# A three-part kernel on one core: the compare of a float64 cast moved to its first steps, and steps among the expert units laid out anew

## The chip, the cores and the metric

The kernel runs on one core of a Trainium2 chip. The core has a matrix engine (PE, whose weight loads are listed as PEld), a vector engine (DVE), an activation engine (ACT) and a general engine (POOL), which run side by side, each through its own list of instructions in order, and wait for each other by semaphores. A fifth one (SP) issues nearly all DMA transfers, also in order. The metric is the device time of one execution in microseconds (us), lower is better.

## The reference

The computation has three parts, one behind the other:

```python
# 1: attention in chunks of 32 queries over 56 keys near them and 8 memory keys (4 batches, 8 heads, 768 positions, 64 wide)
a = np.exp(scores - np.max(scores, axis=-1, keepdims=True)); a = a / (np.sum(a, axis=-1, keepdims=True) + 1e-09)
out[:, :, c_start:c_end] = np.matmul(a, v_full)
# 2: soft mixture of 8 experts with 4 slots each, x is 3072 x 512
logits = x @ phi
d = softmax(logits, axis=0);  slot_input = d.T @ x
h = np.maximum(slot_input[e] @ w1[e], 0.0);  slot_out[e] = h @ w2[e]       # for each expert e, 512 -> 1024 -> 512
c = softmax(logits, axis=1);  x = c @ slot_out
# 3: a layer with a soft gate and a normalisation
h = x @ w_in                                  # w_in is drawn in float64, 512 x 1024
solu = h * softmax(h);  ln = (solu - mean) / np.sqrt(var + 1e-06) * g_ln
return (ln @ w_out).astype(np.float32)        # w_out is drawn in float64, 1024 x 512
```

`softmax` is written out in the reference as in the first part. `w_in` and `w_out` come to the chip as float64, in 16 chunks of 512 KB, and are made into float32 there.

## The kernel before, in words

**Stages.** The first loop goes over 32 groups `g` of attention (two heads, half a batch). In each, PE multiplies queries and keys (L237), DVE takes maxima and differences (L255, L260), ACT the exponential (L269), PE turns the result (L274), ACT copies it (L277), PE multiplies with the values (L297), DVE divides (L263). POOL, ACT and DVE spread keys and values into padded buffers (`move`, L281 to L285). Every four groups one block of tokens is complete, and its logits, the running column maximum and the slot inputs follow (`emit_lg` to `emit_dacc`, L316 to L369). The second loop goes over 32 *units* `n`: one unit is half of an expert's first product (`emit_w1`, L447, eight matmuls) or of its second (`emit_w2`, L465, eight matmuls). The third stage turns the slots into the layer's 24 blocks of tokens and ends in long rows of products (L680, L690).

**A unit.** ACT copies a first product out (L448), PE turns it (L454), DVE adds up parts (L457), POOL applies the relu (L458); this is `emit_ht`, and it stands behind the first product of the next expert half, two units later. The second product of that half comes three units after its turn. Each unit uses two weight chunks of 512 KB. Weights flow into some 27 slots; `load_e` issues what fits, and `release` returns a slot when its last reader has been issued.

**A cast.** One float64 chunk is 128 x 512 pairs of words. From the high word, DVE shifts the exponent and mantissa bits into float32 form (`bits`, L523), puts in sign and top exponent bit (`more`, L529) and keeps the power of two alone (`power`, L534); ACT turns the low word into a number (L526) and squares the high word read as float32 (L535); POOL multiplies low word and power (L538 or L542) and adds (L539 or L545); DVE sets the result to zero where the square is under a threshold (`flush`, L552). For `w_out` ACT then scales by `g_ln` and rounds to the high part (L569), and DVE takes the rest as a low part (L573). Six of the eight `w_in` chunks are cast in the attention loop, one step a group (`casts`), a seventh around its end (`tail`), the eighth and all of `w_out` in the second loop: a new cast starts every three units (`LANE`), and each unit does the next step of every cast begun (`lane`).

**The combine weights.** The row softmax of the logits is done in four batches `b` of six blocks (`combine`). Its steps are: maximum and difference (DVE L405, POOL L406), exponential (ACT L409), sum, inverse and product (DVE L412 to L414, POOL L415), a rounded high part (ACT L418; for the first batch with a turn of its own, DVE L388, PE L392, ACT L393), the low part (POOL L422), and turns on PE with ACT's copies (`emit_c4t`, L438, L439). The list `cb` holds them, one step a unit from unit `SIDE`; each batch's turn is put `CLATE` places further down.

**Order.** Every engine does its instructions in the order in which the program emits them; a step that waits holds all that stand behind it on its engine. Within a unit that is: the unit's product, the turn of an earlier one, the cast steps, SP's loads, a combine step.

Of the kernel before, what the change touches and what calls it, by code (L numbers as in the profile page):

```python
# [12 lines left out]
ACTF = mybir.ActivationFunctionType  # L13
ALU = mybir.AluOpType
# [27 lines left out]
CAST0, CASTN, NEARLY = 3, 4.5, 6  # L42
VLEAD = 3
LOADS = [0] + [1, 1, 1, 0] * 8
LANE, SIDE = 3, 2
C_ID, C_I4, C_REP, C_NM, C_PHI, C_G = 0, 128, 160, 288, 289, 417
NCONST = 425
NPE, NZ = 4, 4
# [11 lines left out]
SPL = 3  # L60
LAG = 2

CLATE = 2
TORD = [1, 0]
TKEEP = [2, 1]
KEEP = (4, 2, 0, 10)
# [5 lines left out]
TINY = (2.0 ** -15 * 1.125) ** 2  # L72
# [3 lines left out]
def tile_kernel(ctx: ExitStack, tc: tile.TileContext, kr, vr, w1, w2, w_in, w_out, cst, out):  # L76
    nc = tc.nc
    pe, dve, act, pool, sp = nc.tensor, nc.vector, nc.scalar, nc.gpsimd, nc.sync
# [9 lines left out]
    def area(tag, regions):  # L88

        total = 0  # L90
        for name, n in regions:
            total = (total + 31) // 32 * 32
            arenas[name] = [total, n, None]
            total += n
        tl = sb.tile([P, total], FP32, name=regions[0][0] + "_area", tag=tag)
        for name, _ in regions:
            arenas[name][2] = tl
# [16 lines left out]
    def at(name, off, n, dt=FP32):  # L114
        o, size, tl = arenas[name]
        assert off + n <= size, (name, off, n, size)
        v = tl[:, o + off:o + off + n]
        return v if dt == FP32 else v.bitcast(dt)
# [3 lines left out]
    def bank(i):  # L122
        return banks[i]
# [32 lines left out]
    w_in_f = at("win", 0, KC * FF)  # L156
# [41 lines left out]
    slot_of = {}  # L198
# [6 lines left out]
    def load_e(n=99):  # L205
        while n and nxt[0] < len(chunks):
            key = chunks[nxt[0]]
            if key[0] == "wout":
                slot = wslot[key[1]]
            elif free:  # L210
                slot = free.pop(0)
            else:
                break
            slot_of[key] = slot
            if key[0] in ("w1", "w2"):
                src = (w1 if key[0] == "w1" else w2)[key[1], key[2]]
                sp.dma_start(out=slot.rearrange("p (k f) -> p k f", k=2), in_=src)
            else:
                src = (w_in if key[0] == "win" else w_out)[key[1]]
                sp.dma_start(out=slot.bitcast(I64), in_=src)  # L220
            nxt[0] += 1
            n -= 1

    def release(key):
        free.append(slot_of[key])
# [169 lines left out]
    def combine(b):  # L395

        l = L[:, TB * b:TB * b + TB, :]
        m, z = cm[:, TB * (b % 2):TB * (b % 2) + TB], cs[:, TB * (b % 2):TB * (b % 2) + TB]
        l2 = l.rearrange("p t (o s) -> p t o s", o=1).to_broadcast([P, TB, 2, NSLOT])

        def wide(x):
            return x.rearrange("p (t o) -> p t o", o=1).to_broadcast([P, TB, NSLOT])

        def top():
            dve.tensor_reduce(out=m, in_=l, axis=AX.X, op=ALU.max)  # L405
            pool.tensor_tensor(out=l, in0=l, in1=wide(m), op=ALU.subtract)  # L406

        def ex():
            act.activation(out=l, in_=l, func=ACTF.Exp)  # L409

        def norm():
            dve.tensor_reduce(out=z, in_=l, axis=AX.X, op=ALU.add)  # L412
            dve.tensor_scalar(out=z, in0=z, scalar1=1e-9, scalar2=None, op0=ALU.add)
            dve.reciprocal(out=z, in_=z)  # L414
            pool.tensor_tensor(out=l, in0=l, in1=wide(z), op=ALU.mult)  # L415

        def hi():
            act.copy(out=c4_of(b)[:, :, 0:2, :], in_=l2)  # L418

        def lo():  # L420
            c4 = c4_of(b)
            pool.tensor_tensor(out=c4[:, :, 2:4, :], in0=l2, in1=c4[:, :, 0:2, :].bitcast(FP32), op=ALU.subtract)  # L422

        return [top, ex, norm, hi if b else lambda: (emit_c0(), hi()), lo, lambda: emit_c4t(b)]
# [25 lines left out]
    def emit_ht(e, half):  # L450
        n = 2 * e + half
        tp = bank(2 + n % 2)
        for j in range(4):
            pe.transpose(out=tp[:, j * P:j * P + P], in_=hr[n % 2][:, j * P:j * P + P], identity=ident)  # L454
        h = ht[e][:, 4 * half:4 * half + 4, SE * e:SE * e + SE]
        parts = tp.rearrange("p (j k s) -> p j s k", j=4, k=KC)[:, :, SE * e:SE * e + SE, :]
        dve.tensor_reduce(out=h, in_=parts, axis=AX.X, op=ALU.add)  # L457
        pool.tensor_scalar(out=h, in0=h, scalar1=0.0, scalar2=None, op0=ALU.max)  # L458
# [11 lines left out]
    def keep_clock(o, n):  # L470

        for _ in range(n):
            pe.matmul(out=o, lhsT=c4t(0), rhs=whi[0], start=True, stop=True)
# [38 lines left out]
            out=m4[:, sl], in0=mhi[:, sl].bitcast(FP32), scalar=nmask, in1=m_of(half), op0=ALU.mult, op1=ALU.add  # L512
        )

    def cast_ops(raw, t2, dst, apart=False):
        w32 = raw.bitcast(I32).rearrange("p (n w) -> p n w", w=2)
        lo = raw.bitcast(U32).rearrange("p (n w) -> p n w", w=2)[:, :, 0]
        lf, hf = (raw.rearrange("p (n w) -> p n w", w=2)[:, :, i] for i in range(2))
        hi = w32[:, :, 1]
        di, t2i = dst.bitcast(I32), t2.bitcast(I32)  # L520

        def bits():
            dve.tensor_scalar(  # L523
                out=di, in0=hi, scalar1=3, scalar2=0x3FFFFFFF, op0=ALU.logical_shift_left, op1=ALU.bitwise_and
            )
            act.activation(out=lf, in_=lo, func=ACTF.Copy, scale=2.0 ** -52)  # L526

        def more():
            dve.scalar_tensor_tensor(  # L529
                out=di, in0=hi, scalar=-0x40000000, in1=di, op0=ALU.bitwise_and, op1=ALU.bitwise_or  # L530
            )

        def power():
            dve.tensor_scalar(out=t2i, in0=di, scalar1=-0x800000, scalar2=None, op0=ALU.bitwise_and)  # L534
            act.activation(out=hf, in_=hf, func=ACTF.Square)  # L535

        def low(eng=pool):
            eng.tensor_tensor(out=t2, in0=lf, in1=t2, op=ALU.mult)  # L538
            eng.tensor_tensor(out=dst, in0=dst, in1=t2, op=ALU.add)  # L539

        def low_a():
            pool.tensor_tensor(out=t2, in0=lf, in1=t2, op=ALU.mult)  # L542

        def low_b():
            pool.tensor_tensor(out=dst, in0=dst, in1=t2, op=ALU.add)  # L545

        def flush(eng=dve):
            if eng is pool:
                pool.tensor_scalar(out=hf, in0=hf, scalar1=TINY, scalar2=None, op0=ALU.is_ge)
                pool.tensor_tensor(out=dst, in0=hf, in1=dst, op=ALU.mult)  # L550
                return
            dve.scalar_tensor_tensor(out=dst, in0=hf, scalar=TINY, in1=dst, op0=ALU.is_ge, op1=ALU.mult)  # L552

        return [bits, more, power] + ([low_a, low_b] if apart else [low]) + [flush]

    def win_ops(j, t):

        sl = slice(512 * j, 512 * j + 512)
        ops = cast_ops(slot_of["win", j], at("tmp", 512 * (t % 2), 512), w_in_f[:, sl], apart=True)
        return ops[:-1] + [lambda: (ops[-1](), release(("win", j)))]  # L560

    def wout_ops(j, t):

# [191 lines left out]
    with tc.manual_schedule():  # L755
# [67 lines left out]
        emit_lcopy(HB - 2)  # L823
        emit_softmax(GROUPS + 2)
        tail = win_ops(NEARLY, NEARLY)
        tail[0]()
        tail[1]()
# [26 lines left out]
            f()  # L854
        load_e()
        cb = [x for b in range(NTILE // TB) for x in combine(b)]
        cb.append(lambda: None)
        for i in range(5, len(cb), 6):
            x = cb.pop(i)
            cb.insert(i + CLATE, x)  # L860
        area("x1", [("wo2", 3 * DM)])
# [8 lines left out]
        after = []  # L870
        lane = []
        waiting = [lambda t, j=j: win_ops(j, t) for j in range(NEARLY + 1, 2 * KC)]
        waiting += [lambda t, j=j: wout_ops(j, t) for j in range(FC)]
        for n, u in enumerate(units):
            if u == units[-1]:
                keep_clock(bank(5), KEEP[0])
            (emit_w1 if u[0] == "w1" else emit_w2)(*u[1:])
            after.append(u[1:] if u[0] == "w1" else None)
            if len(after) > 1 and after[-2] and (LAG == 1 or after[-2][0] == 0):
                emit_ht(*after[-2])  # L880
            if LAG == 2 and len(after) > 2 and after[-3] and after[-3][0]:
                emit_ht(*after[-3])
            for j in range(2):
                release(u[:2] + (2 * u[2] + j,))
            if n % LANE == 0 and waiting:
                lane.append(waiting.pop(0)(n // LANE))
            for q in list(lane):
                q.pop(0)()
                if not q:
                    lane.remove(q)  # L890
            load_e()
            if n >= SIDE and cb:
                cb.pop(0)()
# [108 lines left out]
```

## Time and profile before

| what | value |
|---|---|
| runs | 351.29 us median of 3 (350.53 to 351.62) |
| profiled execution | 351.6 us, its span 349.8 us |
| busy: PE, DVE, ACT, POOL | 308.8, 249.1, 238.9, 221.1 us |
| PE's last block of work (L680) | 130.4 us |
| HBM | 80.11 MB read, 16.78 MB written |

The span runs from the first to the last instruction. Times in the views are from the span's start. A duration holds what an instruction waited for within itself; a time in brackets is idle time of the engine before it, with what ended it. The attention loop and its tail go to 124 us, the 32 units to 189 us, and the third stage to the end.

### The profile page before, as it was taken

How to read it: one execution, taken by the hardware profiler on the slowest of the kernel's cores; microseconds unless marked ns; L12 is line 12 of the kernel's file. 1: busy time of each engine (PE TensorE's matmuls, PEld its weight loads, DVE VectorE, ACT ScalarE, POOL GpSimd, SP SyncE). 2: the span in 40 equal slices, each digit the busy share in tenths (PEclk: the TensorE clock that was granted, in tenths of full speed). 3: DMA queues.
4: the chain of work that ended last, by engine and by line, in shares of the span. 5: the costliest groups of instructions: out<-in, count | busy, mean ns of one | idle time of the engine just before them, and what ended most of it. 6: DMA issues, size and time to landing. Idle time of an engine off the chain costs nothing.

```text
span 349.8 us, 8154 instructions
## 1 busy us (share of the span) xinstructions
PE 308.8 (88%) x2968; PEld 215.8 (62%) x2968; DVE 249.1 (71%) x445; ACT 238.9 (68%) x437; POOL 221.1 (63%) x413
## 2 busy tenths in 40 slices
PE   2988799899988796756769999999999999999996
PEld 1765566666665341221224578888888888888885
DVE  4696988989897754765732598686988698788540
ACT  2678777977875553554642578987998789799631
POOL 5588797886984256587671056787667477567600
PEclk9999999999999999999969999999999999999999
DMA  7999999999999999999910001576665766576621
GB/s 275 414 414 414 413 408 415 407 389 382 334 414 412 418 379 410 415 420 417 410 42 3 0 0 75 197 238 214 207 248 176 258 219 246 195 259 212 240 90 60
DMA packets 38919, 97.41 MB, mean 278 GB/s; under 512 B 4320, under 2 KB 14944, under 8 KB 38880
## 3 DMA queue, kind: packets, MB, share of 16 engines
q1 hardware_dynamic: 38736, 96.68, 72.6%
q8 instruction: 23, 0.38, 0.4%
q10 hardware_dynamic: 144, 0.22, 0.3%
q14 instruction: 16, 0.13, 0.1%
HBM read 80.11 MB, written 16.78 MB: 277 GB/s over the span
## 4 chain that ended last, share of the span: by engine, by line
PE 58%; DVE 14%; POOL 11%; ACT 6%; DMA 6%; issue 3%; SPq 0%; POOLq 0%; ACTq 0%; DVEq 0%
PE bank L680 35%; DMA kq_area<-in_kr_dram 6%; PE h L592 3%; PE bank L297 3%; POOL cst_area L538 2%; POOL hr_area L458 2%; PE bank L447 2%; POOL wo_area L539 2%; POOL v_area L285 2%; PE bank L465 2%; DVE wo_area L552 1%; PE bank L316 1%; PE bank L237 1%; PE bank L358 1%; DVE cst_area L529 1%
## 5 line engine op out<-in xcount | busy, mean ns | idle before, releaser
L680 PE MATMUL bank<-wh_area,yh_area 128*128 128x512 f32 x552 | 130.4, 391 | 0.0
L680 PEld LDWEIGHTS bank<-wh_area,yh_area 128*128 128x128 f32 x552 | 103.4, 188 | 22.4
L285 POOL TENSOR_SCALAR v_area<-v_area 64x780 f32<-64x780 f32 x64 | 57.1, 892 | 17.2 <-issue 5.3
L663 DVE STREAM_TRANSPOSE yq_area<-yq_area 128x1024 f32<-128x1024 f32 x20 | 24.9, 1245 | 23.0 <-DMA yq_area<-z 23.0
L237 PE MATMUL bank<-kq_area 128*32 128x128 f32 x768 | 29.5, 290 | 8.2 <-ACT kq_area L281 6.8
L297 PE MATMUL bank<-v_area,s_area 128*32 128x130 f32 x768 | 28.5, 281 | 8.9 <-ACT s_area L277 3.3
L646 POOL TENSOR_SCALAR cst_area<-cst_area 128x1 f32<-128x1 f32 x72 | 27.9, 388 | 7.1
L607 DVE SCALAR_TENSOR_TENSOR eb_area<-h,eb_area 128x1024 f32<-128x1024 f32 x24 | 28.8, 1203 | 4.5 <-ACT eb_area L601 4.2
L598 DVE TENSOR_REDUCE cst_area<-h 128x1 f32<-128x1024 f32 x24 | 29.0, 1216 | 3.9 <-PE h L592 3.9
L645 POOL TENSOR_SCALAR cst_area<-cst_area 128x1 f32<-128x1 f32 x72 | 25.6, 356 | 7.7
L670 ACT CAST yh_area<-yq_area 128x1024 fp32r<-128x1024 f32 x20 | 21.0, 1050 | 13.3 <-DVE yq_area L663 13.1
L297 PEld LDWEIGHTS bank<-v_area,s_area 128*32 128x32 f32 x768 | 20.3, 110 | 14.4 <-POOL v_area L285 4.7
L237 PEld LDWEIGHTS bank<-kq_area 128*32 128x32 f32 x768 | 20.3, 114 | 14.1 <-ACT kq_area L281 9.1
L601 ACT ACTIVATE eb_area<-h,cst_area 128x1024 f32<-128x1024 f32 x24 | 26.6, 1108 | 1.3 <-DVE cst_area L598 1.3
L630 ACT ACTIVATE eb_area<-eb_area,cst_area 128x1024 f32<-128x1024 f32 x24 | 27.3, 1138 | 0.1
L281 ACT COPY kq_area<-kq_area 64x512 f32<-64x512 f32 x39 | 23.7, 608 | 5.3 <-DMA kq_area<-in_kr_dram 5.0
L674 DVE TENSOR_TENSOR yh_area<-yq_area,yh_area 128x1024 fp32r<-128x1024 f32 x20 | 24.6, 1228 | 2.3 <-ACT yh_area L670 2.3
L627 ACT ACTIVATE eb_area<-eb_area,cst_area 128x1024 f32<-128x1024 f32 x20 | 23.1, 1155 | 2.4 <-DVE eb_area L607 1.3
L255 DVE TENSOR_REDUCE cst_area<-bank 128x6 f32<-128x384 f32 x32 | 17.6, 551 | 8.5 <-PE bank L237 8.4
L636 POOL TENSOR_SCALAR cst_area<-cst_area 128x1 f32<-128x1 f32 x24 | 6.3, 264 | 23.7 <-ACT eb_area L630 23.1
L311 ACT COPY s_area<-bank 128x384 f32<-128x384 f32 x32 | 15.2, 478 | 7.5 <-PE bank L308 7.5
L269 ACT ACTIVATE s_area<-s_area 128x384 f32<-128x384 f32 x32 | 16.9, 527 | 3.9 <-DVE s_area L260 3.7
(151 smaller groups left out, 600.8 us busy)
## 6 DMA issues: line engine op xcount, KB each, us to landing
e_area<-in_w_dram SPq DMA_DIRECT2D x42, 512.0 KB, 9.9
kq_area<-in_kr_dram SPq DMA_DIRECT2D x32, 448.0 KB, 6.8
v_area<-in_vr_dram SPq DMA_DIRECT2D x32, 390.0 KB, 7.2
ex_area<-in_w_dram SPq DMA_DIRECT2D x22, 512.0 KB, 9.9
z<-eb_area SPq DMA_DIRECT2D x20, 512.0 KB, 3.0
yq_area<-z SPq DMA_DIRECT2D x80, 128.0 KB, 2.8
out_dram<-eb_area SPq DMA_DIRECT2D x23, 256.0 KB, 2.1
e_area<-in_w_in_dram SPq DMA_DIRECT2D x8, 512.0 KB, 8.2
```

The source lines that it names most:

```text
L237: pe.matmul(out=bk[32 * j:32 * j + 32, t * 128:(t + 1) * 128], lhsT=kq[i][:, KS + c * CH:KS + (c + 1) * CH], rhs=kwin(g % 2, c), start=Tru ...
L285: pool.tensor_scalar(out=o, in0=i, scalar1=1.0, scalar2=0.0, op0=ALU.mult, op1=ALU.add)
L297: pe.matmul(out=bk[32 * j:32 * j + 32, t * 2 * VW:(t + 1) * 2 * VW], lhsT=atb[g % 2][:, c * CH:(c + 1) * CH], rhs=vz[g % 2][:, :, c * VW:( ...
L598: dve.tensor_reduce(out=sc("nm", i), in_=fin["h"][i % 2], axis=AX.X, op=ALU.max, negate=True)
L601: act.activation(out=eb[i % FIN], in_=fin["h"][i % 2], func=ACTF.Exp, bias=sc("nm", i), accum_out=sc("s", i))
L607: dve.scalar_tensor_tensor(out=ub[i % FIN], in0=fin["h"][i % 2], scalar=-1.0 / FF, in1=eb[i % FIN], op0=ALU.mult, op1=ALU.mult, accum_out= ...
L630: act.activation(out=sq, in_=ub[i % FIN], func=ACTF.Square, scale=-float(FF), bias=sc("nu", i), accum_out=sc("vs", i))
L645: pool.tensor_scalar(out=t, in0=r, scalar1=r, scalar2=xx, op0=ALU.mult, op1=ALU.mult)
L646: pool.tensor_scalar(out=r, in0=t, scalar1=1.5, scalar2=r, op0=ALU.add, op1=ALU.mult)
L663: dve.transpose(out=yv[i % FIN].rearrange("p (f a t) -> p a f t", f=FC, a=4), in_=yq[i % FIN].rearrange("p (a f t) -> p a f t", f=FC, a=4),)
L674: dve.tensor_tensor(out=yl[i % FIN][:, sl], in0=tps(i, sl) if i < NPE else yv[i % FIN], in1=yh[i % FIN][:, sl].bitcast(FP32), op=ALU.subtract,
L680: pe.matmul(out=fin["o"][i % 2], lhsT=a[i % FIN][:, f * 128:(f + 1) * 128], rhs=w[f], start=start, stop=stop)
```

## The change

- In a cast, ACT squares the high word first, into the place of the result, and DVE's compare, now the second step, sets the high word itself to zero or keeps it. The bits are taken from that word after. The power of two is taken in the same step as sign and top bit. The last step is POOL's addition; `w_in`'s slot is returned after POOL's product. The number of instructions is the same.
- In the second loop each cast step has its unit written down: `CASTU` gives the units after the cast's first in which the steps are issued. The two DVE steps and POOL's product share the fourth; the scaling stands two units after POOL's addition.
- The combine steps start in unit 1 instead of 2, and a batch's turn stands three places further down instead of two. With the filler steps the last turn is in unit 26 as before.

```diff
-LANE, SIDE = 3, 2
+LANE, SIDE = 3, 1
+
+CASTU = (0, 1, 2, 3, 3, 4, 6, 7)
-CLATE = 2
+CLATE = 3
...
-    def cast_ops(raw, t2, dst, apart=False):
+    def cast_ops(raw, t2, dst):
...
+        def square():
+            act.activation(out=dst, in_=hf, func=ACTF.Square)
+
+        def flush():
+            dve.scalar_tensor_tensor(out=hf, in0=dst, scalar=TINY, in1=hf, op0=ALU.is_ge, op1=ALU.mult)
+
         def bits():
...
-
-        def power():
             dve.tensor_scalar(out=t2i, in0=di, scalar1=-0x800000, scalar2=None, op0=ALU.bitwise_and)
-            act.activation(out=hf, in_=hf, func=ACTF.Square)
...
-        def flush(eng=dve):
...
-            dve.scalar_tensor_tensor(out=dst, in0=hf, scalar=TINY, in1=dst, op0=ALU.is_ge, op1=ALU.mult)
-
-        return [bits, more, power] + ([low_a, low_b] if apart else [low]) + [flush]
+        return [square, flush, bits, more, low_a, low_b]
...
-        ops = cast_ops(slot_of["win", j], at("tmp", 512 * (t % 2), 512), w_in_f[:, sl], apart=True)
-        return ops[:-1] + [lambda: (ops[-1](), release(("win", j)))]
+        ops = cast_ops(slot_of["win", j], at("tmp", 512 * (t % 2), 512), w_in_f[:, sl])
+        return ops[:4] + [lambda: (ops[4](), release(("win", j)))] + ops[5:]
...
-        cb.append(lambda: None)
-        for i in range(5, len(cb), 6):
+        cb += [lambda: None] * (CLATE - 1)
+        for i in range(5, 24, 6):
             x = cb.pop(i)
             cb.insert(i + CLATE, x)
...
             if n % LANE == 0 and waiting:
-                lane.append(waiting.pop(0)(n // LANE))
-            for q in list(lane):
-                q.pop(0)()
-                if not q:
-                    lane.remove(q)
+                for i, f in enumerate(waiting.pop(0)(n // LANE)):
+                    lane.append((n + CASTU[i], f))
+            for x in [x for x in lane if x[0] == n]:
+                x[1]()
+                lane.remove(x)
```

## Rows read from the trace of the kernel before

**Rows 1.** The page's slices, 40 equal ones: the granted clock, GB/s.

```profile
PEclk9999999999999999999969999999999999999999
GB/s 275 414 414 414 413 408 415 407 389 382 334 414 412 418 379 410 415 420 417 410 42 3 0 0 75 197 238 214 207 248 176 258 219 246 195 259 212 240 90 60
```

**Rows 2.** The chain that ended last: start, length, what.

```profile
22.85 8.58 DMA kq_area<-in_kr_dram
...
149.89 1.11 POOL cst_area L538
...
321.79 18.86 PE bank L680 x83
```

**Rows 3.** PE's waits, 123.9 to 189.6: total us, times, longest.

```profile
PE bank L438 <- POOL hr_area L422: 6.9, 4, 2.6
PE bank L454 <- ACT hr_area L448: 4.8, 3, 1.6
PE bank L392 <- DVE hr_area L388: 2.9, 1, 2.9
PE bank L465 <- POOL hr_area L458: 2.7, 6, 0.7
```

**Rows 4.** Two rounds: busy us (instructions) by engine, granted clock, DMA share, GB/s.

```profile
141.47:154.15 12.68, 8.54 (x67) 3.04 (x66) 7.65 (x18) 6.82 (x14) 9.07 (x10) 1.00 1.03 417
154.15:166.83 12.68, 8.55 (x68) 3.05 (x67) 7.65 (x18) 6.87 (x14) 9.07 (x10) 1.00 1.02 417
```

**Rows 5.** DVE's cast steps in order of time: start, duration, line, what.

```profile
149.42 0.41 DVE L523 TENSOR_SCALAR wo_area<-w_area 128x512 int32<-128x512 int32 x1
...
152.38 1.47 DVE L552 SCALAR_TENSOR_TENSOR cst_area<-w_area,cst_area 128x512 f32<-128x512 f32 x1 [2.54 <-POOL cst_area L539]
153.76 0.68 DVE L529 SCALAR_TENSOR_TENSOR wo_area<-w_area,wo_area 128x512 int32<-128x512 int32 x1
...
154.76 0.41 DVE L534 TENSOR_SCALAR cst_area<-wo_area 128x512 int32<-128x512 int32 x1
...
158.97 0.69 DVE L552 SCALAR_TENSOR_TENSOR wo_area<-w_area,wo_area 128x512 f32<-128x512 f32 x1 [2.42 <-POOL wo_area L539]
...
180.16 0.74 DVE L573 SCALAR_TENSOR_TENSOR wh_area<-cst_area,wh_area 128x512 fp32r<-128x512 f32 x1
```

**Rows 6.** POOL in order of time.

```profile
146.23 0.24 POOL L458 TENSOR_SCALAR hr_area<-hr_area 128x16 f32<-128x16 f32 x1
...
148.92 0.96 POOL L458 TENSOR_SCALAR hr_area<-hr_area 128x16 f32<-128x16 f32 x1
...
151.08 1.27 POOL L539 TENSOR_TENSOR cst_area<-cst_area 128x512 f32<-128x512 f32 x1
152.30 0.99 POOL L422 TENSOR_TENSOR hr_area<-cst_area,hr_area 128x384 fp32r<-128x384 f32 x1
154.78 0.75 POOL L406 TENSOR_TENSOR cst_area<-cst_area 128x192 f32<-128x192 f32 x1 [1.49 <-DVE cst_area L405]
...
161.11 0.52 POOL L415 TENSOR_TENSOR cst_area<-cst_area 128x192 f32<-128x192 f32 x1 [1.96 <-ACT w_area L535]
```

**Rows 7.** PE near the end of the units.

```profile
178.68 1.54 PE L438 MATMUL bank<-cst_area,hr_area 128*128 128x128 f32 x6 [2.65 <-POOL hr_area L422]
...
188.43 1.06 PE L465 MATMUL bank<-e_area,hr_area 128*32 128x512 f32 x8
```

**Rows 8.** Stretches of 4 us, columns as in rows 4.

```profile
60.00:64.00 4.00, 4.00 (x74) 3.02 (x78) 3.92 (x12) 2.87 (x8) 3.71 (x4) 1.00 1.02 401
...
176.00:180.00 4.00, 1.35 (x7) 1.14 (x6) 2.29 (x4) 1.18 (x3) 2.55 (x4) 0.69 0.04 17
180.00:184.00 4.00, 4.00 (x20) 0.88 (x19) 0.90 (x2) 1.32 (x4) 3.28 (x3) 0.50 0.00 0
184.00:188.00 4.00, 3.98 (x28) 1.81 (x27) 1.44 (x4) 1.22 (x2) 0.92 (x2) 0.95 0.02 6
```

**Rows 9.** What SP's queue waited for: total us, times, longest.

```profile
SPq L217 <- DVE cst_area L552: 7.0, 1, 7.0
```

More of the change, by code (lines that the diff above doesn't have):

```diff
@@ L531, in more @@
             )
-        def power():
             dve.tensor_scalar(out=t2i, in0=di, scalar1=-0x800000, scalar2=None, op0=ALU.bitwise_and)
-            act.activation(out=hf, in_=hf, func=ACTF.Square)
-        def low(eng=pool):
-            eng.tensor_tensor(out=t2, in0=lf, in1=t2, op=ALU.mult)
-            eng.tensor_tensor(out=dst, in0=dst, in1=t2, op=ALU.add)
         def low_a():
@@ L545, in low_b @@
             pool.tensor_tensor(out=dst, in0=dst, in1=t2, op=ALU.add)
-        def flush(eng=dve):
[L548 to L551, printed above, removed]
-            dve.scalar_tensor_tensor(out=dst, in0=hf, scalar=TINY, in1=dst, op0=ALU.is_ge, op1=ALU.mult)
-        return [bits, more, power] + ([low_a, low_b] if apart else [low]) + [flush]
+        return [square, flush, bits, more, low_a, low_b]
     def win_ops(j, t):
         sl = slice(512 * j, 512 * j + 512)
-        ops = cast_ops(slot_of["win", j], at("tmp", 512 * (t % 2), 512), w_in_f[:, sl], apart=True)
-        return ops[:-1] + [lambda: (ops[-1](), release(("win", j)))]
+        ops = cast_ops(slot_of["win", j], at("tmp", 512 * (t % 2), 512), w_in_f[:, sl])
+        return ops[:4] + [lambda: (ops[4](), release(("win", j)))] + ops[5:]
     def wout_ops(j, t):
```

## The prediction

> **What bounds the kernel now.** I read the page's slices first, then the chain of waits in order of time, then the stretch in which the chain changes engine most often. Three stages show. In the attention stage, to 124 us, the last load on the chain ends at 31.43 us [rows 2]; from there the chain passes between DVE, ACT, POOL and PE, with DVE busy 3.92 us of 4 [rows 8]. In the last stage PE runs one product behind the other, and its last long piece alone is 18.86 us [rows 2]; the change puts nothing there. Between them lie the 32 expert units, and they end when the last eight matmuls do, at 189.49 us [rows 7].
>
> The expert stage looks like a stage that waits for weights, since loads run at 410 to 420 GB/s through it. But they are over in the slice that begins at 174.9 us with 42 GB/s [rows 1]: 42/415 of 8.745 us is 0.9, so the last lands near 175.8, and PE ends 13.7 us after that. The stage runs on buffered weights, and something else sets its pace.
>
> That is seen in a round of six units (two casts, one batch of combine weights). It takes 12.68 us twice over; PE works 8.54 us of it, DVE 7.65, ACT 6.82, POOL 9.07 [rows 4]. No engine is full, so a loop through several is the bound. PE's waits name it [rows 3]: 6.9 us for POOL's low part of the combine weights (L422), 4.8 for ACT's copy of the first product (L448), 2.9 for the first turn (L388) and 2.7 for POOL's relu (L458), 17.3 together. Behind these is the cast: DVE's compare (L552) waits for POOL's two steps, ACT's scaling for the compare, and the copy that PE needs is behind the scaling in ACT's queue.
>
> A second thing is in the durations. DVE's compare takes 0.69 us at 158.97, but 1.47 at 152.38, where POOL's L422 began 0.08 us before it [rows 5, 6]; it ends 0.56 us after L422's end, so it was held until POOL was nearly done. The other way round POOL's relu takes 0.24 us at 146.23 and 0.96 at 148.92, ending at 149.88, just after DVE's L523, which ended at 149.83. DVE's cast steps and POOL exclude each other. The Trainium skill says the same (SBUF — State Buffer, Who interferes with whom): DVE and GpSimd share a port pair, a DVE instruction with two SBUF inputs or in a two-port mode takes it, and the loser blocks for a whole instruction. The 0.78 us more agree with it.
>
> Last, a clock loss. PE waits 2.65 us until 178.68 [rows 7], and the granted clock is 0.69 in 176 to 180, 0.50 in 180 to 184 and 0.95 in 184 to 188 [rows 8], which is the lower level, 1.2 GHz, until about 184.4. From 178.68 to there PE does 5.7 us at half speed: 2.8 us lost.
>
> **The change part by part.** *The compare first.* A cast has the same eight instructions as before: on DVE 0.41 + 0.68 + 0.41 + 0.69 and, for w_out, 0.74 us [rows 5]; on ACT the square and the low word; on POOL two products. The compare now writes the strided high word, which no row shows. The nearest rows are this kind of instruction with a strided operand on the reading side, 0.68 (L529) and 0.69 (L552); the far ones are 0.41, DVE's shortest cast step, and 1.47, the blocked compare. I take 0.69; at 1.47 four rounds of two casts would cost 6.2 us more, which stays among the two in ten left out. What is gained is order: nothing on DVE waits for POOL's result any more. DVE's wlo waits for ACT's scaling of the unit before. The new wait, compare on square, has a whole unit (2.1 us) or attention group of cover; in the tail, where both are issued together, DVE next has a step that waits for PE anyway. Without cover it is 0.7 us a cast.
>
> *Eight units.* The scaling stands two units after POOL's last step instead of one after a compare that itself waits, so ACT's queue stops there for nothing and the 4.8 us of copy waits should nearly go. What is late next is POOL: the first product is issued in the unit of the two DVE steps that feed it, and the relu of a later unit queues behind it. PE feels a relu only when it comes three units late.
>
> *Combine weights.* The turn (PE) follows the low part by four units instead of three, the last by three instead of two. All steps but the turns start one unit sooner. That takes the 6.9 us of L422 waits to about nothing, but the time is not free: the port may fill it.
>
> *So count the port.* Undisturbed, a round holds on DVE 2 x 2.93 = 5.9 us, on POOL two products at 1.1 and 1.27 us (L538 on the chain [rows 2], L539), three relus at 0.24, 0.52 for each combine product (L415; the 0.75 of L406 I take as holding a wait) and 0.99 for L422: 7.5 [rows 6]. That is 13.4 us in a round of 12.68, so the instructions overlap at their ends. Laid over each other, POOL's 9.07 us and the ten cast steps of DVE in a round (the last is L552 at 152.38, the next round's first L529 at 153.76 [rows 5]) cover 11.8 us: 2.7 of DVE's stand beside an idle POOL. So 0.9 us a round is free on both, time in which each waited for an engine outside. A little more overlap comes from DVE's steps now standing side by side. I take 11.7 us a round, 1.0 less; the bounds are 12.7 (no gain) and 10.7 (as much again through overlap).
>
> The sum is made from the 351.6 us of the profiled execution (span 349.8 and 1.8 around it). Four rounds at 1.0 give 4.0 us (bounds 0 and 8). Of the first turn's wait of 2.9 us, one unit sooner and with no compare ahead of it on DVE, I take 0.9 (0 to 2.9). The last turn waits 2.65 us where the other three take 1.4 on average ((6.9 - 2.6)/3 [rows 3]); a round's share of that is in the first term, and of the other 1.2 I take 0.9. The clock gives back 2.8 (0 to 2.8) if no gap so long stands before the last units. In the tail of the attention the slot of w_in's seventh chunk is free after POOL's first product instead of the compare; SP stood 7.0 us for it [rows 9], but weights are not the bound, so that is nothing; one DVE step less on the way to unit 0 is 0.3 (-0.5 to 0.7). In the attention loop the six early casts keep their groups and instructions; one port wait more or less is 0.8 us (1.47 - 0.69), and I allow two of them on the chain: 0, within 1.5. W_out's last step is issued in unit 31 instead of 30, 0.74 us beside PE's last turn: nothing, and 0.74 if that cover is gone.
>
> Together 8.9, so 342.7 us. The runs' median, 351.29, is 0.3 under this execution; I leave that out.
>
> **The rivals.** First: *The clock falls anyway* (345.5). PE still works under three quarters of a round, and a relu that is late makes gaps like the old ones. For it: one gap of 2.65 sufficed. Against: the one of 2.9 before the first turn did not [rows 3], and gaps should be shorter. Chance 0.17.
>
> Second: *The port is the bound already* (346.7). Instructions and their port time are unchanged; if a blocked POOL loses as much as the loop gave, the round stays at 12.7 and the 4.0 go. For it: 13.4 us of port work in 12.68. Against: the 0.9 us free on both. Chance 0.12. The Trainium skill's rule of an exclusive lock (the same section), taken strictly, speaks for this rival; the trace agrees as far as the 0.78 us by which the compare was held.
>
> Third: *PE meets the loads* (339.1 to 341). If overlap is better, unit 31 still can't run before 175.8; with its own 1.06 us PE ends near 177, and 12.5 us are gained at most. Chance 0.09.
>
> Fourth: *The relu starves* (slower). Place: POOL's queue in the expert stage. DVE's compare, first bits and wlo now stand in a row, 1.8 us; behind them POOL's product of 1.1 is held, and the relu behind that; DVE's next pair can hold it again, 1.1. If a relu is over 4.3 us late (three units at PE's 8.54/6), PE stops for it. Two stops of 2.7 us more a round, over four rounds, cost 21.6 and outweigh the 17.3 of waits that are there now: 355.9. It decides from 17.3/8 = 2.2 us a stop if all the old waits went. Against: POOL gets the port whenever DVE waits, and it has 3.6 us of free time in a round. Chance 0.07.
>
> Fifth: *No change that can be measured*: losses in attention eat the gain, 350.5 to 352.5. Chance 0.05.
>
> **How the numbers follow.** The forecast has 0.50, with 341 to 344.5 as its own range. 339.5 to 347.0 holds it, rival 1, most of 2 and of 3: a little over 0.8. A difference of 0.3%, 1.05 us, is about what a measurement tells from none. Faster: 0.50 + 0.17 + 0.12 + 0.09 = 0.88; same 0.05; slower 0.07.
>
> **What would show it.** Right: rounds of 11.4 to 12 us in the middle of the expert stage; PE's waits for L422 and L448 under 1 us each, those for the relu grown to 5 or more; the compare at 0.7 us except where POOL holds it; clock 1.00 from 176 to 188; PE's last expert matmuls ending near 180.5; the last stage as long as before. Wrong: an expert stage that begins over 1.5 us later than before, a round still at 12.7, or a strided compare of over 1 us alone on the port.

## The result and the profile after

The changed kernel takes 345.57 us (median of 4 runs, 344.54 to 347.21) against 350.98 us (4 runs, 350.53 to 351.62) of the kernel before on the same chip: ratio 0.9849, 95% interval 0.9803 to 0.9895. A later repetition gave 0.9824 (0.9796 to 0.9853). The forecast was 342.7, with 341 to 344.5 as its own range; the measured time lies outside that and where the first rival put it (345.5). The profiled execution took 346.21 us with a span of 344.4; before, 351.6 and 349.8.

Lines have new numbers. The compare L552 is now L529, the bits L523 are L532, sign and exponent L529 are L538, POOL's two products L538/L542 and L539/L545 are L544 and L547, the relu L458 is L460, ACT's copy L448 is L450, the second product L465 is L467, the combine turn L438 is L440, its low part L422 is L424, and the first turn L392 after L388 is L394 after L390.

The difference by stage, each point read from the start of the same PE instruction in both traces (units are counted from 0):

The prediction does not say where its four rounds lie; here two of them are put to units 10 to 21 and two behind.

| stretch | before, us | after, us | difference | forecast |
|---|---|---|---|---|
| attention and routing, to unit 0 | 123.95 | 122.27 | -1.7 | -0.3 |
| units 0 to 9 | 17.52 | 17.50 | 0.0 | -0.9 |
| units 10 to 21, two rounds | 25.36 | 22.23 | -3.1 | -2.0 |
| unit 22 to the last matmul of the units | 22.66 | 22.35 | -0.3 | -5.7 |
| the third stage | 160.32 | 160.07 | -0.2 | 0 |

The page's slices after (granted clock, GB/s), beside [rows 1]:

```profile
PEclk9999999999999998999888999999999999999999
GB/s 273 413 413 414 411 411 414 414 411 401 345 416 409 417 417 410 412 420 418 409 82 0 0 31 93 193 252 173 265 214 204 241 263 185 212 246 225 233 93 61
```

The one deep clock digit of before has become four shallow ones, and the dip to 379 GB/s of the fifteenth slice is gone. That dip was the 7.0 us of [rows 9]; SP's wait for the cast slot is now in three parts, the longest 2.8:

```profile
SPq L219 <- POOL cst_area L544: 6.1, 3, 2.8
```

PE's waits from 120 to 192 us (total us, times, longest), beside [rows 3]:

```profile
PE bank L467 <- POOL hr_area L460: 8.8, 8, 2.1
PE bank L394 <- DVE hr_area L390: 2.4, 1, 2.4
PE bank L456 <- ACT hr_area L450: 1.1, 4, 0.3
```

The 6.9 us for the combine weights are gone, the copy fell from 4.8 to 1.1, and the relu rose from 2.7 to 8.8. The same rounds as in [rows 4], by unit number (10 to 15, 16 to 21, 22 to 27):

```profile
139.77:149.86 10.09, 8.43 (x68) 3.04 (x67) 9.85 (x15) 6.15 (x12) 9.43 (x10) 1.00 1.03 415
149.86:162.00 12.14, 8.61 (x67) 3.05 (x67) 11.97 (x19) 6.70 (x13) 10.93 (x11) 1.00 1.03 418
162.00:174.55 12.55, 9.91 (x67) 4.00 (x70) 12.38 (x20) 8.75 (x17) 11.26 (x11) 0.86 0.97 388
```

DVE had 7.65 us busy of 12.68 before; now 11.97 of 12.14. Its cast steps are the same in number; the rest is time in which it is held within its instructions. DVE in order of time in the second of these rounds (start, duration, line), beside [rows 5]:

```profile
154.20 0.73 DVE L568 SCALAR_TENSOR_TENSOR wh_area<-cst_area,wh_area 128x512 fp32r<-128x512 f32 x1
154.86 1.78 DVE L529 SCALAR_TENSOR_TENSOR w_area<-wo_area,w_area 128x512 f32<-128x512 f32 x1
156.68 0.43 DVE L532 TENSOR_SCALAR wo_area<-w_area 128x512 int32<-128x512 int32 x1
157.02 0.22 DVE L459 TENSOR_REDUCE hr_area<-bank 128x16 f32<-128x64 f32 x1
157.15 1.74 DVE L538 SCALAR_TENSOR_TENSOR wo_area<-w_area,wo_area 128x512 int32<-128x512 int32 x1
```

And POOL, beside [rows 6]:

```profile
154.29 1.80 POOL L544 TENSOR_TENSOR cst_area<-w_area,cst_area 128x512 f32<-128x512 f32 x1 [0.42 <-DVE hr_area L459]
156.06 0.68 POOL L460 TENSOR_SCALAR hr_area<-hr_area 128x16 f32<-128x16 f32 x1
156.71 1.54 POOL L547 TENSOR_TENSOR wo_area<-wo_area,cst_area 128x512 f32<-128x512 f32 x1
158.20 1.56 POOL L424 TENSOR_TENSOR hr_area<-cst_area,hr_area 128x384 fp32r<-128x384 f32 x1
```

Read them together. POOL's product begins at 154.29, while DVE's L568 runs to 154.93, and ends at 156.09. DVE's compare begins at 154.86 and ends at 156.64, 0.55 us after that product. DVE's L538 ends at 158.89, 0.64 us after POOL's L547. Each of the two engines stands in the other's time, and the relu of 0.24 us [rows 6] stands behind both: 0.68. PE feels that at the places below, beside [rows 7] (the first turn, the second product, the second product again):

```profile
131.25 0.33 PE L394 MATMUL bank<-cst_area,hr_area 128*128 128x128 f32 x1 [2.44 <-DVE hr_area L390]
156.80 1.06 PE L467 MATMUL bank<-e_area,hr_area 128*32 128x512 f32 x8 [1.56 <-POOL hr_area L460]
168.94 1.11 PE L467 MATMUL bank<-ex_area,hr_area 128*32 128x512 f32 x8 [1.56 <-POOL hr_area L460]
179.26 1.19 PE L467 MATMUL bank<-e_area,hr_area 128*32 128x512 f32 x8 [2.09 <-POOL hr_area L460]
```

The waits before 131.25, 168.94 and 179.26 are followed by a clock fall each, about 3.4 us at the lower level (1.2 GHz); the one before 156.80 is not. In stretches of 4 us, beside [rows 8]:

```profile
132.00:136.00 4.00, 4.00 (x28) 1.23 (x23) 0.47 (x2) 2.02 (x4) 1.76 (x3) 0.57 1.03 410
168.00:172.00 4.00, 3.06 (x18) 0.80 (x19) 3.93 (x6) 1.55 (x4) 4.00 (x5) 0.73 1.02 408
180.00:184.00 4.00, 4.00 (x20) 2.11 (x16) 0.88 (x2) 0.72 (x1) 1.12 (x2) 0.57 0.01 4
```

In the two profiled executions there was one fall of 6.8 us before, and there are three after, 10.2 us together; other executions of the changed kernel had fewer or more (see "The clock"). The third stage's long piece on the chain is as long as in [rows 2]:

```profile
316.61 18.86 PE bank L675 x83
```

### The profile page after: what moved, and what is told of

Read it like the earlier page. It is cut to its first block, busy times and chain, and to the rows that moved or that the text cites. A ratio compares the mean times of both kernels' runs of the same rounds, so it can differ in the third digit from the quotient of the medians.

```text
span 344.4 us, 8169 instructions
## 1 busy us (share of the span) xinstructions
PE 309.9 (90%) x2968; PEld 217.0 (63%) x2968; DVE 262.3 (76%) x445; ACT 238.3 (69%) x437; POOL 224.5 (65%) x413
## 4 chain that ended last, share of the span: by engine, by line
PE 54%; DVE 20%; ACT 6%; issue 3%; POOL 2%; ACTq 0%; DVEq 0%; POOLq 0%
PE bank L675 35%; PE h L587 3%; DVE w_area L529 3%; PE bank L299 2%; DVE wh_area L568 2%; DVE cst_area L538 1%; DVE wo_area L538 1%; PE bank L449 1%; DVE wo_area L532 1%; PE bank L310 1%; ACT kq_area L283 1%; PE bank L318 1%; DVE cst_area L541 1%; PE bank L467 1%; PE bank L456 1%
## 5 line engine op out<-in xcount | busy, mean ns | idle before, releaser
L640 POOL TENSOR_SCALAR cst_area<-cst_area 128x1 f32<-128x1 f32 x72 | 27.7, 384 | 7.7
L641 POOL TENSOR_SCALAR cst_area<-cst_area 128x1 f32<-128x1 f32 x72 | 25.0, 347 | 7.1
L631 POOL TENSOR_SCALAR cst_area<-cst_area 128x1 f32<-128x1 f32 x24 | 6.4, 267 | 24.2 <-ACT eb_area L625 23.5
L693 ACT ACTIVATE eb_area<-bank,cst_area 128x512 f32<-128x512 f32 x23 | 15.7, 681 | 5.4 <-POOL cst_area L631 3.4
```

The source lines that it names most:

```text
L640: pool.tensor_scalar(out=t, in0=r, scalar1=r, scalar2=xx, op0=ALU.mult, op1=ALU.mult)
L641: pool.tensor_scalar(out=r, in0=t, scalar1=1.5, scalar2=r, op0=ALU.add, op1=ALU.mult)
```

## Experiments

All ratios are against the kernel before, timed on the same chip, with 95% intervals. "The changed kernel" is the base of an edit unless "the kernel before" is named.

**The parts alone.** The casts alone (the kernel before with the new cast and `CASTU`; `SIDE` and `CLATE` stay at 2, the list `cb` as it was):

```diff
-    def cast_ops(raw, t2, dst, apart=False):
+    def cast_ops(raw, t2, dst):
...
+                    lane.append((n + CASTU[i], f))
```

> The casts as in the changed kernel (attention, tail and units), the combine steps and their turns where they were before. Theory A (what counts is that DVE no longer waits for POOL): most of the 5.4 us stay, 346.5 to 348.5 us; PE's waits for ACT's copy of the first product fall from 4.8 to about 1 us, those for POOL's low part of the combine weights stay near 5. Rival B (what counts is the later turn of the combine weights, PE's largest wait before, 6.9 us): 349.5 to 351.

347.39 us, ratio 0.9861 (0.9831 to 0.9892), 4.9 us less. PE's waits in the units:

```profile
PE bank L440 <- POOL hr_area L424: 4.6, 3, 2.2
PE bank L456 <- ACT hr_area L450: 4.5, 6, 1.5
```

The copy waits stayed at 4.5 us of 4.8. So the new order of the cast alone does not take them away; with the combine steps earlier they go to 1.1.

The combine weights alone (the kernel before):

```diff
-LANE, SIDE = 3, 2
+LANE, SIDE = 3, 1
-CLATE = 2
+CLATE = 3
...
-        cb.append(lambda: None)
-        for i in range(5, len(cb), 6):
+        cb += [lambda: None] * (CLATE - 1)
+        for i in range(5, 24, 6):
```

> The combine steps start in unit 1 and turn three units behind their last step; the casts are as before. Theory A: 348.5 to 350.5 us, since DVE's compare still waits for POOL and holds up the copies; the 6.9 us of waits for the low part go to under 2, but those for the copy or the relu grow. Rival B: 345.5 to 347.

349.03 us, ratio 0.9911 (0.9881 to 0.994), 3.1 us less. A round of six units (columns as in [rows 4]):

```profile
150.14:162.96 12.82, 8.61 (x68) 3.05 (x67) 8.03 (x17) 6.71 (x13) 9.32 (x11) 1.00 1.03 418
```

And PE's waits:

```profile
PE bank L465 <- POOL hr_area L458: 8.6, 7, 2.2
PE bank L454 <- ACT hr_area L448: 4.6, 7, 1.2
```

The turn no longer waits for L422, the relu does in its place, and this round is no shorter. What the turn's place gives is won in units 0 to 15 (26.39 us against 30.20 before); behind unit 22 part of it is lost again (24.89 us against 22.66, with clock falls of 10.2 us in all).

The new cast in the attention loop and its tail alone (the kernel before; the casts among the units stay):

```diff
-                    early[j] = win_ops(j, j)
+                    early[j] = win_new(j, j)
...
-        tail = win_ops(NEARLY, NEARLY)
+        tail = win_new(NEARLY, NEARLY)
```

> The new order of a cast in the attention loop and its tail alone; the units are those of the kernel before. The changed kernel began its units 1.7 us sooner, where 0.3 was forecast. If the order of the cast steps makes that, units begin 1.2 to 2.0 us sooner here too and the time is 349 to 350 us. If it came with the units' own change (slots, loads) or by chance of one execution, units begin within 0.5 us of before and the time is 350.5 to 351.5.

350.5 us, ratio 0.9948 (0.9924 to 0.9972), 1.8 us less; unit 0 begins at 121.80 us, and PE's waits in the units are those of [rows 3]. The reverse, the changed kernel with the old cast there:

```diff
-                    early[j] = win_ops(j, j)
+                    early[j] = win_old(j, j)
...
-        tail = win_ops(NEARLY, NEARLY)
+        tail = win_old(NEARLY, NEARLY)
```

> The old order of a cast in the attention loop and its tail, the changed kernel's casts and combine steps among the units. If the attention part of the change is worth 1.7 us, this is 347 to 347.8 us; if it is worth nothing, 345 to 346. Rounds of six units at 12.1 us as in the changed kernel, by both.

347.89 us, ratio 0.9878 (0.9847 to 0.991); unit 0 at 123.44. So about 1.7 of the 5.4 us come before the first unit, where the forecast had 0.3. (In the profiled execution of the repetition below, with a clock fall from 29 to 33 us, unit 0 begins at 123.24: one fall takes 1.0 of it back.) The combine steps 3.1, the casts among the units 3.1 (4.9 - 1.8) and those in attention 1.8 make 8.0, and together they gave 5.4 to 6.2. Each of these differences carries about 1 us either way, so that it is likely and not shown that the parts don't add up.

**Is the port what stops the round?** The square and the shifted bits go to a bank of PSUM, so that DVE's compare, first bits and sign step have one operand less in SBUF. Bank 5 is taken from the first turn, and two steps of the cast come one unit earlier:

```diff
-CASTU = (0, 1, 2, 3, 3, 4, 6, 7)
+CASTU = (0, 1, 1, 2, 3, 4, 6, 7)
...
-            act.activation(out=dst, in_=hf, func=ACTF.Square)
+            act.activation(out=mid, in_=hf, func=ACTF.Square)
...
-            dve.scalar_tensor_tensor(out=hf, in0=dst, scalar=TINY, in1=hf, op0=ALU.is_ge, op1=ALU.mult)
+            dve.scalar_tensor_tensor(out=hf, in0=mid, scalar=TINY, in1=hf, op0=ALU.is_ge, op1=ALU.mult)
...
-        waiting += [lambda t, j=j: wout_ops(j, t) for j in range(FC)]
+        waiting += [lambda t, j=j: wout_ops(j, t, bank(5)[:, 0:512]) for j in range(FC)]
```

> The changed kernel, but among the units the square and the shifted bits go through a PSUM bank instead of the place of the result, so that three of a cast's five DVE steps have at most one SBUF tensor input; sign bits and power one unit earlier; the first turn uses another bank. Theory (DVE and POOL exclude each other on a port, and that is what bounds a round): the compare takes 0.7 to 0.8 us instead of up to 1.8, POOL's first product 1.1 to 1.3 instead of 1.8, the round falls from 12.1 to about 10.5, time 340 to 343 us. Rival (the strided compare is slow by itself, or DVE is simply full): compare still 1 to 1.8 us, round 11.8 to 12.5, time 345 to 347.

338.62 us, ratio 0.9632 (0.9602 to 0.9661), 13.5 us less. The same round, units 16 to 21:

```profile
150.06:159.62 9.56, 8.47 (x67) 3.04 (x66) 9.21 (x18) 6.67 (x14) 8.82 (x11) 1.00 1.03 418
```

DVE's cast steps and POOL's products beside each other:

```profile
152.79 0.71 DVE L530 SCALAR_TENSOR_TENSOR w_area<-bank,w_area 128x512 f32<-128x512 f32 x1
153.54 0.70 DVE L533 TENSOR_SCALAR bank<-w_area 128x512 int32<-128x512 int32 x1
154.27 0.69 DVE L539 SCALAR_TENSOR_TENSOR wo_area<-w_area,bank 128x512 int32<-128x512 int32 x1
154.99 1.26 DVE L542 TENSOR_SCALAR cst_area<-wo_area 128x512 int32<-128x512 int32 x1
```

```profile
153.21 1.31 POOL L545 TENSOR_TENSOR cst_area<-w_area,cst_area 128x512 f32<-128x512 f32 x1
154.69 1.27 POOL L548 TENSOR_TENSOR wo_area<-wo_area,cst_area 128x512 f32<-128x512 f32 x1
```

POOL's product runs from 153.21 to 154.52, and three DVE steps with an operand in PSUM go by it at 0.69 to 0.71 us. The fourth, from SBUF to SBUF, meets POOL's L548 and takes 1.26 where it takes 0.41 alone [rows 5]. PE's waits for the relu fell from 8.8 to 2.0 us:

```profile
PE bank L467 <- POOL hr_area L460: 2.0, 5, 0.5
```

Since this kernel also has the earlier steps, a control has those without PSUM (`CASTU` and the bank of the first turn as there, nothing else):

```diff
-CASTU = (0, 1, 2, 3, 3, 4, 6, 7)
+CASTU = (0, 1, 1, 2, 3, 4, 6, 7)
...
-        pe.transpose(out=bank(5)[:, 0:128], in_=rep4, identity=ident)
-        act.copy(out=c0t, in_=bank(5)[:, 0:128])
+        pe.transpose(out=bank(6)[:, 0:128], in_=rep4, identity=ident)
+        act.copy(out=c0t, in_=bank(6)[:, 0:128])
```

> Control to the run with the PSUM bank: the same re-timing (bits one unit after the square, sign bits and power two after, the first turn in the other bank), but square and bits in the place of the result as in the changed kernel. Theory (the port made the gain of that run): rounds of about 12 us, compares up to 1.8 us, 344.5 to 347. Rival (the re-timing made it): a round under 10.5 us, 338 to 341.

342.97 us, ratio 0.973 (0.9699 to 0.9761), between the two times that were expected.

```profile
150.20:161.96 11.76, 8.61 (x67) 3.04 (x67) 11.41 (x18) 6.70 (x13) 11.02 (x11) 1.00 1.03 419
```

```profile
PE bank L467 <- POOL hr_area L460: 8.6, 9, 1.4
```

Its interval lies apart from both neighbours', so two things are shown. The earlier steps are worth 3.3 to 4.2 us (0.973 against 0.9824 and 0.9849), and PSUM a further 3.4 (0.9632 against 0.973). PSUM shortens the round from 11.76 to 9.56 us. With the earlier steps DVE and POOL are as full as before, and the relu waits are as long in sum, but none is over 1.4 us, and the one clock fall of this execution stands at the first turn. Unit 22 begins at 161.96 in it and at 162.00 in the changed kernel, and the units end at 181.75 against 184.35: the 2.6 us arise behind unit 22, where the changed kernel has two falls and this one none. Executions with a mean granted clock of 0.993 to 0.995 took 343.50 to 343.77 us here, 338.31 to 340.82 with PSUM, and the only such one of the changed kernel 344.85. So PSUM's gain is not one of the clock; of that of the earlier steps a good part seems to be.

Last, POOL's two products left out of the nine casts among the units (so the low words of those chunks are missing from the weights):

```diff
-        return [square, flush, bits, more, low_a, low_b]
+        return [square, flush, bits, more] + ([low_a, low_b] if low else [lambda: None] * 2)
```

> The changed kernel without POOL's two products in the nine casts among the units, so the low parts of these weights are left out. Theory (port): every DVE compare takes 0.7 us, DVE's and POOL's waits go, a round falls to PE's own 8.6 to 9.5 us, PE meets the loads in the last units and the time is 338 to 340.5. Rival (strided compare slow by itself): compares of 1 us and more stay, round above 10.5, time 342 or more.

338.82 us, ratio 0.9637 (0.9608 to 0.9666).

```profile
145.53:153.80 8.27, 8.27 (x68) 3.04 (x67) 7.88 (x18) 6.83 (x15) 4.48 (x6) 1.00 1.03 418
```

```profile
PE bank L449 <- DMA e_area<-in_w_dram: 0.9, 4, 0.2
```

PE is full in this round and meets the loads, and the units end at 177.03. With PSUM the products are all there, and the time is the same within the intervals.

**The relu's queue.** If the relu only stands in the wrong queue, DVE can do it:

```diff
-        pool.tensor_scalar(out=h, in0=h, scalar1=0.0, scalar2=None, op0=ALU.max)
+        dve.tensor_scalar(out=h, in0=h, scalar1=0.0, scalar2=None, op0=ALU.max)
```

> The changed kernel with the experts' relu on DVE, right behind the sum that it follows, instead of on POOL. PE waited 8.8 us for the relu. Theory (the relu stands in POOL's queue behind a product that DVE blocks): PE's waits for it fall under 4 us, time 342.5 to 344.5. Rival (the relu is late because DVE's sum before it is late, behind a blocked compare): the waits move to DVE's line and stay at 6 to 9 us, time 345 to 346.5.

350.19 us, ratio 0.9947 (0.9927 to 0.9966): some 4 us slower than the changed kernel. The theory falls; the waits are the rival's, but the time is beyond both.

```profile
PE bank L467 <- DVE hr_area L460: 7.6, 8, 1.9
PE bank L456 <- ACT hr_area L450: 4.1, 4, 1.4
```

```profile
156.10 1.31 POOL L544 TENSOR_TENSOR cst_area<-w_area,cst_area 128x512 f32<-128x512 f32 x1 [0.43 <-DVE hr_area L459]
156.12 1.32 DVE L460 TENSOR_SCALAR hr_area<-hr_area 128x16 f32<-128x16 f32 x1
...
161.15 0.17 DVE L460 TENSOR_SCALAR hr_area<-hr_area 128x16 f32<-128x16 f32 x1
```

The same instruction takes 0.17 us or 1.32: on DVE, too, it is held, here until POOL's product ends, and PE's waits for the copies rose from 1.1 to 4.1 us.

**The clock.** Idle products on constants hold PE busy in the gaps: four ahead of the first turn, one ahead of each second product from the eighth unit:

```diff
+    def hold(n):
+        for _ in range(n):
+            pe.matmul(out=bank(5)[:, 0:GTOK], lhsT=ident, rhs=at("cst", 0, GTOK), start=True, stop=True)
...
+            if u[0] == "w2" and n >= 7:
+                hold(1)
```

> The changed kernel with idle products on PE, four ahead of the first turn of the combine weights and one ahead of each second product from unit 7, where PE waited. Theory (the granted clock fell three times after such waits and cost some 4 us): no fall before the end, clock 1.00 through the units, time 342 to 344. Rival (the falls hid under waits for POOL that come anyway, so they cost little): clock 1.00 but time 345 to 346.5, with the waits for the relu grown by what the products no longer lack.

344.24 us, ratio 0.9786 (0.976 to 0.9812); the granted clock is 1.00 through all units.

```profile
149.66:160.80 11.14, 10.35 (x73) 3.86 (x72) 10.97 (x17) 6.12 (x12) 9.92 (x10) 1.00 1.03 419
```

By the ratios this is 1.3 to 2.2 us under the changed kernel, whose repetition follows:

> The changed kernel itself, in as many rounds as the experiments, since its first interval (0.980 to 0.990) touches that of the run with idle products on PE. Theory (the clock falls cost some 2 us): ratio 0.982 to 0.987, above 0.9786. Rival (they cost nothing): 0.977 to 0.980.

346.5 us, ratio 0.9824 (0.9796 to 0.9853). The intervals of 0.9786 and 0.9824 still touch, and the round is 11.14 us at a clock of 1.00 where it was 12.14 at 1.00, so that not all of it is the clock. From this pair alone the price of the falls is not settled. The changed kernel's nine executions go further, since their mean granted clock (in the table to the nearest 0.005) differs. The profiled one, with 10.2 us at the lower level, has 0.984, so a step of 0.005 stands for about 3.4 us:

| mean granted clock | time, us |
|---|---|
| 0.995 | 344.85 |
| 0.99 | 344.54, 344.94, 346.39 |
| 0.985 | 346.21, 346.50, 346.94, 347.21 |
| 0.98 | 348.53 |

A straight line through the nine gives 1.3 us for each step. The trace of the repetition shows one step by itself. The round of units 22 to 27 has no fall in it, behind the same wait of the relu as at 168.94 above, and takes 11.54 us instead of 12.55:

```profile
169.97 1.06 PE L467 MATMUL bank<-ex_area,hr_area 128*32 128x512 f32 x8 [1.57 <-POOL hr_area L460]
163.03:174.57 11.54, 8.49 (x67) 3.16 (x70) 11.37 (x18) 8.51 (x17) 10.33 (x10) 1.00 1.00 401
```

So a fall of 3.4 us costs some 1.0 to 1.3 us, three of them 3.0 to 3.9, and whether one comes behind a given wait differs between executions of one kernel.

**What binds next.** With PSUM, loads and slots should be the bound. First, loads laid closer:

```diff
-LOADS = [0] + [1, 1, 1, 0] * 8
+LOADS = [0] + [1, 1, 1, 0] * 4 + [1, 1, 1, 1] + [1, 2, 1, 1] + [1, 1, 1, 1] * 2
```

> The kernel with the PSUM bank, with four more weight chunks issued in the last twelve attention groups, where loads ran under 400 GB/s for some 25 us. Theory (with the port freed PE meets the loads: the last weight landed at 176.0 us and PE ended the units at 177.3): the last weight lands 2 to 3 us sooner, 335.5 to 337.5 us. Rival (engines still bound the units, or the chunks delay the keys and values of attention by as much): 338 to 340.

338.63 us, ratio 0.962 (0.9589 to 0.965), no change. From 84 to 88 us the loads went from 332 to 411 GB/s as meant, but SP then waited for slots before the units:

```profile
84.00:88.00 4.00, 4.00 (x96) 2.95 (x84) 3.71 (x11) 3.38 (x9) 2.58 (x3) 1.00 1.03 411
...
124.00:128.00 4.00, 4.00 (x36) 1.41 (x32) 2.86 (x8) 2.97 (x7) 1.27 (x4) 1.00 0.96 350
```

```profile
SPq L219 <- POOL cst_area L545: 8.9, 3, 4.4
```

The last weights landed 0.8 us sooner (an estimate from the traces: about 175.2 after 176.0). The same with four idle products before the first turn:

```diff
+        for _ in range(4):
+            pe.matmul(out=bank(6)[:, 0:GTOK], lhsT=ident, rhs=at("cst", 0, GTOK), start=True, stop=True)
```

> As the kernel with the PSUM bank and the four early chunks, with four idle products on PE ahead of the first turn, where the clock fell for 6.8 us. Theory (PE meets the loads at the end, so that what is lost in the middle is slack): same as without them within 0.7 us, though the clock stays at 1.00. Rival (the fall still costs): 1.5 to 3 us less than without them.

338.48 us, ratio 0.9613 (0.9581 to 0.9645). The clock is 1.00 and the units end at 176.43, where they ended at 176.55 with a fall: here the fall costs nothing that can be measured. With the fall PE's weight loads waited 2.3 us for the units' weights, without it 5.0: the time comes back as a wait for loads. The three PSUM kernels, at 338.5 to 338.6 us, beat both kernels of this case.

## Why the prediction was right or wrong

**Right: the order and what is late next.** The kernel is faster because DVE no longer waits for POOL's result and the turns come later. The waits for L422 and the copy went from 11.7 to 1.1 us, and the relu's rose to 8.8 where "5 or more" was forecast. The casts and the combine steps alone show that it takes both. Of the prediction's other signs, the rounds of 11.4 to 12 us, the clock of 1.00 from 176 to 188 and the end of the units near 180.5 did not come: 10.09 and 12.14, 0.57 in 180 to 184, and 184.35.

**The four rounds (4.0): too coarse.** The two middle rounds gave 3.1 us, where half of the term is 2.0, but as 10.09 and 12.14 us, and not 11.7 twice. The shorter one holds 25 instructions of DVE and POOL, the second 30, and in the second nothing is free: both engines are in an instruction nearly all the time. The round of 11.7 counted on more overlap at the ends of the instructions; in the steady round the held time ate it. The port's sum was also too low: the 1.1 us for POOL's product is a piece of the chain and not the instruction, which took 1.43 us there (149.57 to 151.00) and 1.31 beside the PSUM steps; with 1.31 the sum is 13.8 us, not 13.4. The second rival named the right resource, and the PSUM kernel against its control shows it: with the same steps in the same units the round goes from 11.76 to 9.56. The Trainium skill (SBUF — State Buffer, Who interferes with whom) says that a DVE instruction with at most one SBUF input and outside the two-port modes doesn't contend with GpSimd; the steps of 0.69 to 0.71 us beside POOL's 1.31 agree. The 1.26 us of the step that stays in SBUF, which has one input as well, agrees only if that step runs in such a mode, which no run here shows.

**The clock (2.8): the step that failed, and with it the forecast's size.** It was to come back "if no gap so long stands before the last units". Gaps of 2.09 and 1.56 us were enough, both for the relu that the prediction itself had called late. From unit 22 to the end the units gained 0.3 us of the 5.7 forecast (2.0 for the rounds, 0.9 for the last turn, 2.8 for the clock). Rival 1 had said so, at 0.17; it deserved more, since the forecast's own next wait stood before both falls. By the figures above the three falls of the profiled execution cost an estimated 3.0 to 3.9 us, about what the forecast is off by. The two behind unit 22 are 2.0 to 2.6 of the 5.4 us missing there, and without its fall the round of units 22 to 27 takes 11.54 us, near the forecast's 11.7; the rest of the 5.4 was not separated.

**The first turn (0.9): 0.5, and taken back.** Its wait went from 2.94 to 2.44 us, a clock fall followed it (0.57 in 132 to 136), and units 0 to 9 stayed where they were (17.50 us; 17.21 with the idle products and no fall, so the fall seems to be only part of it). That the old gap of 2.9 had not lowered the clock was used as evidence against rival 1. It was one execution: with the new cast in attention alone, in units like those of before, the clock did fall behind that gap (2.93 us until 132.26; 0.57 in 132 to 136).

**The tail and attention (0.3 and 0): too small.** 1.7 us came, shown by the exchange of that cast alone (1.8) and its reverse. SP's wait at the slot went from 7.0 us in one piece to a longest of 2.8; which of the seven casts gave how much was not tried. This gain was not foreseen, and that the measured time falls on rival 1's 345.5 is in part luck: without the 1.4 us beyond the forecast it would be 347.0.

**The last stage** stayed within 0.2 us, as forecast, and the strided compare of the changed cast took 0.69 us, as taken, in the kernel without POOL's products among the units (one group of it: total us, mean ns):

```profile
L529 DVE SCALAR_TENSOR_TENSOR w_area<-cst_area,w_area 128x512 f32<-128x512 f32 x2 | 1.4, 686 | 0.0
```

The sum: -1.4 us from attention and -1.1 from the two middle rounds beside the forecast, +0.9 from units 0 to 9, +5.4 behind unit 22, -0.2 from the last stage make +3.6, which is 346.2 - 342.7 within rounding.

## What to carry to other kernels

When two engines hold each other within their instructions, reordering takes idle time away only until one of them is in an instruction all the time; then look for an operand that can stand in PSUM, and compare the durations beside each other in the timeline. Before you count on a clock that comes back, ask which wait is late next: the clock fell behind a wait of 1.56 us here, where the old one had been 2.65. Look at the granted clock of several executions: one profiled execution does not tell whether a fall belongs to the kernel. Try a part in its own place as well as in the whole: the parts here summed to 8.0 us and gave 5.4 to 6.2, though that difference is hardly clear of noise.

## What the runs showed of the hardware

- Clock falls of about 3.4 us followed PE waits of 1.56, 2.09 and 2.44 us, and one of 6.8 us followed a wait of 2.65 [rows 7, 8]; another wait of 1.56, before 156.80, had none. Nor does the place decide: behind the wait of 1.56 before 168.94 the clock fell, behind that of 1.57 at the same place of the repetition it did not. What decides, no run here settles.
- A tensor-scalar step from SBUF into PSUM took 0.70 us, from SBUF into SBUF 0.43 us. The dearer one stands in the faster kernel: it kept its 0.70 beside POOL's product, while a step from SBUF into SBUF (0.41 alone) took 1.26 there.
- Where DVE has steps one behind the other, POOL's relu (0.24 us) took 0.68. DVE's own version of it took 0.17, or 1.32 beside POOL's product of 1.31: a small instruction can pay the whole length of the large one beside it.
